# A retention and two expert layers on one core: the slots of the first layer's ranked experts worked out over six steps of the first job, where one step held them all

## The chip, the core and the metric

The kernel runs on one core of a Trainium2 chip. The metric is device time in microseconds (us), the median of several runs. Engines are named as the profile names them: PE is TensorE, DVE is VectorE, ACT is ScalarE, POOL is GpSimd, SP is the engine that issues most transfers. PEld is PE's loading of weights.

## What is computed

A linear attention with decay (2 x 8 heads, 768 positions, 64 wide) gives 1536 tokens of 512 numbers. Two layers of eight experts follow. Each token goes to its two best experts in the first layer, weighted by a softmax of the two logits, and to its best one in the second, up to a capacity:

```python
noisy_logits = x @ w_gate + np.log1p(np.exp(x @ w_noise)) * noise
top2 = np.argpartition(-noisy_logits, 2, axis=1)[:, :2]
...
h = np.maximum(x[mask] @ w1[e], 0.0)
out[mask] += top2_w[mask, k, None] * (h @ w2[e])
```

In the second layer `expert_idx = np.argmax(x @ w_gate, axis=1)`, and the output of the expert is multiplied by the softmax probability.

## The kernel before, in words

The core works through jobs. A job is one expert with a number of its tokens: it gathers their rows by an indirect DMA from POOL, turns them by PE transposes (`tr`, L730), splits them into a high and a low part (L731 on ACT, L732 on DVE), and multiplies by split weights, three matmuls (L740, L741, L742) for each product of two tiles. A job of the first kind has nine steps. In step f PE sums eighth f + 1 of the first product into a PSUM bank `hp` (12 matmuls here), ACT takes its relu (L814), DVE takes the relu's low part (L815, which the change's title calls a relu too), and PE adds eighth f of the second product into `yp` (12 matmuls again). The matmuls L741 of the second product read what L815 wrote. `experts` runs these steps, and behind each step calls `extra1(j, i)` with the job's and the step's number, where other work can be put in.

The first layer's job 0 is expert 0 with up to 288 of the tokens of the first nine tiles, whose choice is known early. Job 1 is expert 0 with up to 128 tokens of the rest. Jobs 2 to 8 are the other seven experts, ranked by the number of their tokens, with 408 to 372 slots each. Which token stands in which of these slots is worked out by `slots`: for 24 groups of 128 choices (12 tiles of tokens, two choices each) DVE finds rank and row of every choice and spreads the values to be placed over the columns that they may go to (`sel`, L433, then one large product, L442). 24 short instructions (L445, called marks below) set a one-hot tile for each group. 24 small matmuls (L447) then add the groups up, beginning with the last group. That is done twice, once for the tokens' numbers (into `tr`, from `more`) and once for their weights (from `oh`, in `rest`). DVE turns the sums into `Rsrc` and `Rdst`, by which POOL gathers and scatters, and `Rwt`.

All of this was in `late()`, called behind step 1 of job 0. Instructions carry priorities, and the engines' orders are set by them when the program is built: on the chip each engine takes its own list strictly in order. `tc.issue_after(tail[...])` ranks what stands in it behind the last instruction of that kind.

Two buffers matter. `flat`, which holds `sel` and the ranks, is the same buffer as `yT`, into which ACT and DVE copy a job's output when it ends (L876, L874, before the matmuls L892). `tr` has two banks, used in turn by transposes, by L892 and by both runs of L447.

Of the kernel before, what the change touches and what calls it, by code (L numbers as in the profile page):

```python
# [14 lines left out]
OP = mybir.AluOpType  # L15
# [22 lines left out]
def kernel(ctx: ExitStack, tc: tile.TileContext, q, k, v, lam, g1, gn, noise,  # L38
# [375 lines left out]
    def slots(nm, rank, row, nh, flat, lows_, first_, last_, choices, tag, past):  # L414
# [5 lines left out]
        for x, w in (("ge", nh + 1), ("up", 1), ("lo", 1), ("hi", nh), ("ro", RANKED), ("sel", C)):  # L420
# [3 lines left out]
        nc.vector.tensor_tensor(ge, rank[:, :, None].to_broadcast([P, K, nh + 1]),  # L424
                                steps_p[:, None, :nh + 1].to_broadcast([P, K, nh + 1]), op=OP.is_ge)
        nc.vector.tensor_reduce(up[:, :, 0], ge, axis=AX.X, op=OP.add)

        nc.vector.scalar_tensor_tensor(lo[:, :, 0], up[:, :, 0], -float(P), rank, op0=OP.mult, op1=OP.add)
        nc.vector.tensor_scalar(lo[:, :, 0], lo[:, :, 0], P + 1.0, None, op0=OP.add)
        nc.vector.tensor_sub(hi, ge[:, :, :nh], ge[:, :, 1:])  # L430
        nc.vector.tensor_tensor(ro, row[:, :, None].to_broadcast([P, K, RANKED]),
                                e_up[:, None, :RANKED].to_broadcast([P, K, RANKED]), op=OP.is_equal)
        nc.vector.tensor_tensor(sel.rearrange("p k (r h) -> p k r h", h=nh),  # L433
                                ro[:, :, :, None].to_broadcast([P, K, RANKED, nh]),
                                hi[:, :, None, :].to_broadcast([P, K, RANKED, nh]), op=OP.mult)
        src, dst, wt = small(nm + "src", [P, C], I32), small(nm + "dst", [P, C], I32), small(nm + "wt", [P, C])

        def columns(values, rhs, make):
            f = values.shape[2]
            rhs = rhs[:, :K * f * C].rearrange("p (k f c) -> p k f c", k=K, f=f)  # L440
            ps = bank(tag, [P, 3, RANKED * 4])[:, :f, :C]
            nc.vector.tensor_tensor(rhs, sel[:, :, None, :].to_broadcast([P, K, f, C]),  # L442
                                    values[:, :, :, None].to_broadcast([P, K, f, C]), op=OP.mult)
            for k in range(K if make else 0):
                nc.vector.tensor_scalar(lows_(k), slot1[:, :P], lo[:, k, :], None, op0=OP.is_equal)  # L445
            for i, k in enumerate([K - 1, *range(K - 1)]):
                nc.tensor.matmul(ps, lows_(k), rhs[:, k], start=(i == 0), stop=(i == K - 1))  # L447
            return ps

        ps = columns(first_[0], first_[1], True)  # L450
        t, ch, d = (small("sl" + x, [P, 2 * NT + 4])[:, :C] for x in "tcd")
        nc.vector.tensor_copy(t, ps[:, 1])
        nc.vector.scalar_tensor_tensor(d, t, 0.0, past, op0=OP.is_equal, op1=OP.max)
        nc.vector.tensor_scalar(d, d, 2.0 * NO_SLOT, None, op0=OP.mult)
        if choices:
            nc.vector.tensor_scalar(ch, t, 16.0, None, op0=OP.is_gt)
            nc.vector.scalar_tensor_tensor(t, ch, -16.0, t, op0=OP.mult, op1=OP.add)
        nc.vector.scalar_tensor_tensor(t, t, float(P), ps[:, 0], op0=OP.mult, op1=OP.add)
        picked = nc.vector.tensor_scalar(src, t, -float(P), 0.0, op0=OP.add, op1=OP.max).ins
        if choices:  # L460
            nc.vector.scalar_tensor_tensor(t, t, 2.0, ch, op0=OP.mult, op1=OP.add)
        nc.vector.scalar_tensor_tensor(dst, t, (-2.0 if choices else -1.0) * P, d, op0=OP.add, op1=OP.add)

        def rest():
            ps = columns(last_[0], last_[1], False)
            nc.vector.tensor_reduce(wt, ps.rearrange("p f c -> p c f"), axis=AX.X, op=OP.add)
# [8 lines left out]
        return of, rest, dst, picked  # L475
# [604 lines left out]
    def late():  # L1080
# [312 lines left out]
```

## Time and profile before

| what | value |
|---|---|
| device time, median of 3 runs | 638.32 us (638.04 to 640.14) |
| the profiled execution, its own time | 643.0 us |
| its span in the trace | 641.2 us |
| mean granted clock of PE over the span | 0.986 |
| PE busy | 603.7 us, 94% of the span |
| DVE busy | 375.1 us, 58% |
| ACT busy | 279.8 us, 44% |
| POOL busy | 175.0 us, 27% |

The profiled execution is one run with the profiler on; the time around its span is 1.8 us. PE's busy time is that of its records. Stretches of the program are named by microseconds from the span's start: the attention fills the time up to about 94 us, job 0 runs from there to 134.8 us, job 1 to about 152 us, the ranked jobs follow, and the second layer begins at about 450 us.

### The profile page before, as it was taken

The numbers are of one execution on the slowest core, as the hardware profiler recorded it, in microseconds if no ns is written. First come the engines' busy times: TensorE is split into PE (matmuls) and PEld (weight loads), VectorE is DVE, ScalarE is ACT, GpSimd is POOL, SyncE is SP. The second block draws the span as 40 slices with busy tenths as digits, with TensorE's granted clock in tenths as the row PEclk, the third lists the DMA queues.
The fourth block names the chain that finished last, engine by engine and source line by source line (L and its number), as shares of the span: only waits on it lengthen the run. The fifth ranks groups of instructions, "written<-read, shape, count | busy, mean of one in ns | idle before, by whom it ended". The sixth has DMA issues, their size and how long they took to land. (4 is left out here: it accounts for less than half of the span.)

```text
span 641.2 us, 11321 instructions
## 1 busy us (share of the span) xinstructions
PE 603.7 (94%) x4173; PEld 562.0 (88%) x4173; DVE 375.1 (58%) x841; ACT 279.8 (44%) x486; POOL 175.0 (27%) x255
## 2 busy tenths in 40 slices
PE   3999989799999999999999999989989999998896
PEld 3898878788999999999999999978669989987795
DVE  3475859736545454464644545447867668557881
ACT  2466531035443353343534434136136357366762
POOL 3844620245004021040310101032255035032101
PEclk9999999799999999999999999999989999999999
DMA  6799522437736447466543421182497977867620
GB/s 151 172 302 270 150 87 86 133 110 253 244 103 211 132 131 231 137 212 183 171 168 98 151 67 51 27 282 84 158 300 244 287 233 227 266 209 239 209 79 33
DMA packets 106048, 110.34 MB, mean 172 GB/s; under 512 B 35855, under 2 KB 81951, under 8 KB 105984
## 3 DMA queue, kind: packets, MB, share of 16 engines
q1 hardware_dynamic: 97920, 83.58, 43.3%
q0 software_dynamic: 8064, 25.95, 12.0%
q8 instruction: 35, 0.57, 0.4%
q14 instruction: 29, 0.24, 0.1%
HBM read 92.48 MB, written 18.79 MB: 174 GB/s over the span
## 5 line engine op out<-in xcount | busy, mean ns | idle before, releaser
L112 DVE TENSOR_TENSOR wl<-wst,wh 128x1024 fp32r<-128x1024 f32 x107 | 135.1, 1270 | 58.1 <-ACT wh L106 56.5
L106 ACT CAST wh<-wst 128x1024 fp32r<-128x1024 f32 x107 | 111.3, 1047 | 32.6 <-PE yp L741 27.1
L740 PE MATMUL hp<-x,wh 128*128 128x372 f32 (+9 forms) x352 | 116.2, 331 | 0.8 <-ACTq L1232 0.4
L741 PE MATMUL hp<-x,wh 128*128 128x372 f32 (+9 forms) x352 | 116.2, 331 | 0.0
L742 PE MATMUL hp<-x,wl 128*128 128x372 f32 (+9 forms) x352 | 115.3, 328 | 0.0
L814 ACT ACTIVATE h<-hp 128x372 fp32r<-128x372 f32 (+9 forms) x88 | 41.2, 469 | 165.6 <-PE hp L742 151.7
L740 PE MATMUL yp<-h,wh 128*128 128x372 f32 (+8 forms) x320 | 106.4, 334 | 1.3 <-ACT h L814 1.3
L742 PE MATMUL yp<-h,wl 128*128 128x372 f32 (+8 forms) x320 | 107.0, 334 | 0.0
L741 PE MATMUL yp<-h,wh 128*128 128x372 f32 (+8 forms) x320 | 106.5, 333 | 0.1
L815 DVE SCALAR_TENSOR_TENSOR h<-hp,h 128x372 fp32r<-128x372 f32 (+9 forms) x88 | 46.5, 528 | 70.3 <-ACT h L814 67.7
L740 PEld LDWEIGHTS hp<-x,wh 128*128 128x128 f32 x352 | 66.2, 188 | 1.9 <-ACTq L1232 0.7
L741 PEld LDWEIGHTS hp<-x,wh 128*128 128x128 f32 x352 | 66.3, 189 | 0.4
L742 PEld LDWEIGHTS hp<-x,wl 128*128 128x128 f32 x352 | 66.2, 188 | 0.1
L490 POOL DMA_INDIRECT xg<-x,Rsrc x25 | 24.3, 971 | 142.0 <-PE tr L730 123.9
L741 PEld LDWEIGHTS yp<-h,wh 128*128 128x128 f32 x320 | 60.8, 190 | 0.7 <-DVE h L815 0.5
L740 PEld LDWEIGHTS yp<-h,wh 128*128 128x128 f32 x320 | 60.0, 188 | 1.5 <-ACT h L814 1.5
L742 PEld LDWEIGHTS yp<-h,wl 128*128 128x128 f32 x320 | 60.7, 190 | 0.3 <-issue 0.2
L732 DVE TENSOR_TENSOR x<-tr,x 128x128 fp32r<-128x128 f32 (+12 forms) x72 | 29.1, 436 | 35.9 <-ACT x L731 35.4
L927 POOL DMA_INDIRECT x<-y,Rdst x25 | 24.9, 998 | 81.7 <-DVE y L901 77.7
L731 ACT CAST x<-tr 128x128 fp32r<-128x128 f32 (+12 forms) x72 | 25.8, 387 | 39.4 <-PE tr L730 38.4
L892 PE MATMUL tr<-iw,yT 128*128 128x136 f32 (+2 forms) x224 | 34.2, 288 | 0.4 <-issue 0.4
L500 POOL TENSOR_TENSOR xg<-xg 128x512 f32<-128x512 f32 (+1 forms) x16 | 22.4, 1403 | 41.0 <-DMA xg<-x,Tsrc 21.6
(370 smaller groups left out, 1036.7 us busy)
## 6 DMA issues: line engine op xcount, KB each, us to landing
wst<-in_moe_w_dram SPq DMA_DIRECT2D x107, 512.0 KB
more<-in_moe_w_dram SPq DMA_DIRECT2D x21, 512.0 KB
ldk<-in_k_dram SPq DMA_DIRECT2D x12, 256.0 KB
ldq<-in_q_dram SPq DMA_DIRECT2D x6, 512.0 KB
ldv<-in_v_dram SPq DMA_DIRECT2D x12, 256.0 KB
x<-xr SPq DMA_DIRECT2D x12, 256.0 KB
out_dram<-zero SPq DMA_DIRECT2D x12, 256.0 KB
dm<-powers SPq DMA_DIRECT2D x1, 512.0 KB
```

The lines of the kernel that those rows point to most:

```text
L106: nc.scalar.copy(hi, st)
L112: nc.vector.tensor_sub(lo, st, hi.bitcast(F32))
L490: i = nc.gpsimd.indirect_dma_start(out=r, out_offset=None, in_=x, in_offset=bass.IndirectOffsetOnAxis(ap=src(s)[:m], axis=0))
L731: a = nc.scalar.copy(hi[:, d, :n], ps[:, :n])
L732: v_ = nc.vector.tensor_sub(lo[:, d, :n], ps[:, :n], hi[:, d, :n].bitcast(F32))
L740: nc.tensor.matmul(ps, a[0], b[0], start=start, stop=False)
L741: nc.tensor.matmul(ps, a[0], b[1], start=False, stop=False)
L742: tail["pe"] = nc.tensor.matmul(ps, a[1], b[0], start=False, stop=stop).ins
L814: tail["act"] = nc.scalar.activation(hh, ps, AF.Relu).ins
L815: tail["dve"] = nc.vector.scalar_tensor_tensor(hl, ps, 0.0, hh.bitcast(F32), op0=OP.max, op1=OP.subtract).ins
L892: nc.tensor.matmul(ps[:m, i, :], self.yT[:, 2 * b + i, s * r:s * r + m], iw[:, 2 * b + i, gates2], start=True, stop=True)
L927: i = nc.gpsimd.indirect_dma_start(out=target, out_offset=bass.IndirectOffsetOnAxis(ap=dst, axis=0), in_=y, in_offset=None, bounds_check=t ...
```

## The change

`slots` no longer runs its parts itself; it returns them as functions: `pick` (ranks, rows and `sel`), `spread` for the first values, `mark` for some of the groups, `head` (the first 24 matmuls and what DVE makes of them), `spread` for the weights, and `rest`. `late(i)` is called behind steps 1 to 7 of job 0 and does one of them at a time; the weights' matmuls come in step 0 of job 1. The second layer calls the same parts one behind the other, in the order that it had.

```diff
-        def columns(values, rhs, make):
+        def spread(values, rhs):
+            f = values.shape[2]
+            return nc.vector.tensor_tensor(view(values, rhs), sel[:, :, None, :].to_broadcast([P, K, f, C]),
+                                           values[:, :, :, None].to_broadcast([P, K, f, C]), op=OP.mult).ins
+
+        def mark(ks):
+            for k in ks:
+                i = nc.vector.tensor_scalar(lows_(k), slot1[:, :P], lo[:, k, :], None, op0=OP.is_equal)
+            return i.ins
+
+        def columns(values, rhs):
             f = values.shape[2]
-            rhs = rhs[:, :K * f * C].rearrange("p (k f c) -> p k f c", k=K, f=f)
             ps = bank(tag, [P, 3, RANKED * 4])[:, :f, :C]
-            nc.vector.tensor_tensor(rhs, sel[:, :, None, :].to_broadcast([P, K, f, C]),
-                                    values[:, :, :, None].to_broadcast([P, K, f, C]), op=OP.mult)
-            for k in range(K if make else 0):
-                nc.vector.tensor_scalar(lows_(k), slot1[:, :P], lo[:, k, :], None, op0=OP.is_equal)
             for i, k in enumerate([K - 1, *range(K - 1)]):
-                nc.tensor.matmul(ps, lows_(k), rhs[:, k], start=(i == 0), stop=(i == K - 1))
+                nc.tensor.matmul(ps, lows_(k), view(values, rhs)[:, k], start=(i == 0), stop=(i == K - 1))
             return ps
...
-        return of, rest, dst, picked
+        return of, dst, pick, lambda: spread(*first_), mark, head, lambda: spread(*last_), rest
...
-        last_rows.append(dst)
-        fetch()
-        fetch()
-        jobs[2].prepare()
-        rest()
-        later1.extend((tot1, rk1))
...
+            fetch()
+            fetch()
+        with tc.issue_after(tail["dve"]), tc.issue_after(tail["pe"]):
+            if i == 2:
+                phases.extend(ranked(later1[1]))
+                phases[2]()
+            if i == 3:
+                phases[3]()
+            if i in (4, 5):
+                phases[4](range(NT) if i == 4 else range(NT, 2 * NT))
+            if i == 6:
+                phases[5]()
+                for r, size in enumerate(FIRST):
+                    jobs.append(Job(("a", r + 1), size, phases[0](r), x1, x2, True, ranked=True))
+                last_rows.append(phases[1])
+                jobs[2].prepare()
+            if i == 7:
+                phases[6]()
...
         if j == 0 and i == 1:
             jobs.append(jobB)
-            late()
+        if j == 0 and 1 <= i <= 7:
+            late(i)
+        if j == 1 and i == 0:
+            with tc.issue_after(tail["pe"]):
+                phases[7]()
```

In the changed kernel the lines have other numbers: L442 is now L446, L445 L451, L447 L458, L740 to L742 are L754 to L756, L815 is L829, L874 L888, L892 L906, L732 L746.

How it moves PE's list, at the place in job 0 where the tokens' matmuls stand. Before, four matmuls of the second product's step 4 (`h_1677`, with `wh12`), then 24 of L447 from `more2` and, right behind, 24 from `oh`:

```order
L740 MATMUL yp0_1323<-h_1677,wh12_82 128x288
L740 MATMUL yp1_1324<-h_1677,wh12_82 128x288
L740 MATMUL yp2_1325<-h_1677,wh12_82 128x288
L740 MATMUL yp3_1326<-h_1677,wh12_82 128x288
L447 LDWEIGHTS more1_1221
L447 MATMUL tr_1487<-more2_1222,more1_1221 128x56
```

Now the rest of that step, the first product's step 6 (`hp_1650`, with `wh03`) and the second product's step 5 (`h_1623`) stand ahead of them, and the first product's step 7 (`hp_1721`) behind; these are the rows around them:

```order
L756 MATMUL hp_1650<-x1_1224,wl03_87 128x288
L754 MATMUL yp0_1323<-h_1623,wh12_82 128x288
L755 MATMUL yp0_1323<-h_1623,wh12_82 128x288
...
L756 MATMUL yp3_1326<-h_1623,wl12_90 128x288
L458 LDWEIGHTS more1_1221
L458 MATMUL tr_1678<-more2_1222,more1_1221 128x56
...
L458 MATMUL tr_1678<-more2_1222,more0_1220 128x56
L754 MATMUL hp_1721<-x1_1224,wh03_79 128x288
```

The 24 matmuls moved back by 32 large ones, of which 8 are the rest of the step that they used to cut in two.

PE's list in job 1, behind the matmuls L906 that finish job 0 (`yT`), where the weights' matmuls now stand (before, only the last L892 and the next matmul stood there):

```order
L906 MATMUL tr_1837<-iw_105,yT_1778 96x136 x2
L756 MATMUL hp_1881<-wh02_78,x0_1223 128x256
L754 MATMUL hp_1881<-wh02_78,x0_1223 128x256
L906 MATMUL tr_1841<-iw_105,yT_1778 96x136 x2
L458 LDWEIGHTS more1_1221
L458 MATMUL tr_1853<-oh_1528,more1_1221 128x84
```

The 24 matmuls from `oh` left job 0 and stand in the middle of job 1's first product.

DVE's list in job 0. Before, all 24 marks and the weights' spread (`oh`) stand ahead of two low parts L815:

```order
L445 TENSOR_SCALAR more1_1221<-slot1_144,yT_1475 128x128
L442 TENSOR_TENSOR oh_1476<-yT_1475,wts_155 128x2016
L452 COPY slt_1537<-tr_1487 128x28
L815 SCALAR_TENSOR_TENSOR h_1677<-hp_1664,h_1677 128x288
L453 SCALAR_TENSOR_TENSOR sld_1539<-slt_1537,past1_161 128x28
L456 TENSOR_SCALAR slc_1538<-slt_1537 128x28
L815 SCALAR_TENSOR_TENSOR h_1705<-hp_1692,h_1705 128x288
```

Now one low part stands ahead of `sel` (L436), one between mark 12 and mark 13, and one behind mark 24; the weights' spread stands behind job 1's splits and ahead of the copies into `yT`:

```order
L829 SCALAR_TENSOR_TENSOR h_1583<-hp_1570,h_1583 128x288
L436 TENSOR_TENSOR yT_1527<-yT_1527 128x672
L451 TENSOR_SCALAR more0_1220<-slot1_144,yT_1527 128x128
L446 TENSOR_TENSOR more2_1222<-yT_1527,who_153 128x1344
...
L829 SCALAR_TENSOR_TENSOR h_1623<-hp_1610,h_1623 128x288
...
L829 SCALAR_TENSOR_TENSOR h_1663<-hp_1650,h_1663 128x288
...
L746 TENSOR_TENSOR x0_1223<-tr_1761,x0_1223 128x128
L446 TENSOR_TENSOR oh_1528<-yT_1527,wts_155 128x2016
L888 COPY yT_1778<-yp1_1324 128x288
```

Three low parts moved ahead of work that they used to stand behind, and the spread of the weights moved behind the last of job 0's low parts.

## Rows read from the trace of the kernel before

**Rows 1.** Windows: span, busy us of each engine (count), granted clock, DMA share, GB/s

```profile
114.76:134.78 20.02, 14.77 (x127) 13.94 (x125) 11.57 (x58) 2.64 (x9) 6.05 (x7) 0.83 0.35 105
134.78:152.00 17.22, 16.96 (x119) 14.79 (x118) 8.27 (x16) 7.81 (x15) 10.47 (x13) 1.00 0.52 169
152.00:450.00 298.00, 295.56 (x1824) 286.33 (x1824) 155.18 (x268) 122.89 (x196) 51.84 (x56) 1.00 0.48 151
```

**Rows 2.** Waits of PE from 80 to 145 us: total, times, longest

```profile
PE tr L447 <- DVE more L445: 3.0, 1, 3.0
PE yp L740 <- ACT h L814: 1.3, 1, 1.3
PE tr L447 <- DVE oh L442: 0.9, 1, 0.9
```

**Rows 3.** Timeline of PE in job 0: start, us, line, tiles, count, idle before

```profile
113.17 0.29 PE L740 MATMUL hp<-x,wh 128*128 128x288 f32 x1
...
114.76 0.69 PE L740 MATMUL yp<-h,wh 128*128 128x288 f32 x4
118.48 1.30 PE L447 MATMUL tr<-more,more 128*128 128x56 bf16 x24 [3.02 <-DVE more L445]
120.64 1.86 PE L447 MATMUL tr<-oh,more 128*128 128x84 bf16 x24 [0.87 <-DVE oh L442]
...
134.78 0.28 PE L740 MATMUL hp<-wh,x 128*128 128x256 f32 x1
...
137.63 1.09 PE L892 MATMUL tr<-iw,yT 128*96 128x136 f32 x8
...
148.17 0.96 PE L730 MATMUL tr<-iw,xg 128*128 128x128 f32 x8
```

**Rows 4.** Windows of 2 us around the wait (columns as in rows 1)

```profile
118.00:120.00 2.00, 1.30 (x24) 1.16 (x24) 2.00 (x4) 0.00 (x0) 0.00 (x0) 0.50 0.00 0
...
124.00:126.00 2.00, 2.00 (x15) 2.00 (x14) 1.09 (x7) 0.00 (x0) 1.39 (x3) 0.83 0.39 94
```

**Rows 5.** Timeline of DVE from 112 to 121 us

```profile
112.20 0.24 DVE L445 TENSOR_SCALAR more<-slot,yT 128x128 bf16<-128x128 f16 x1
112.36 0.85 DVE L433 TENSOR_TENSOR yT<-yT 128x672 f32<-128x672 f32 x1
...
113.29 1.54 DVE L442 TENSOR_TENSOR more<-yT,who 128x1344 bf16<-128x1344 f32 x1
114.76 3.66 DVE L445 TENSOR_SCALAR more<-slot,yT 128x128 bf16<-128x128 f16 x22
118.34 2.25 DVE L442 TENSOR_TENSOR oh<-yT,wts 128x2016 bf16<-128x2016 f32 x1
...
120.60 0.44 DVE L815 SCALAR_TENSOR_TENSOR h<-hp,h 128x288 fp32r<-128x288 f32 x1
```

**Rows 6.** Timeline of ACT: two of job 0's relus and the copies into yT

```profile
111.84 0.41 ACT L814 ACTIVATE h<-hp 128x288 fp32r<-128x288 f32 x1 [5.67 <-PE hp L742]
...
132.04 0.41 ACT L814 ACTIVATE h<-hp 128x288 fp32r<-128x288 f32 x1 [5.33 <-PE tr L730]
...
134.58 0.40 ACT L876 COPY yT<-yp 128x288 f32<-128x288 f32 x1
```

**Rows 7.** Timeline of POOL: the last of job 2's four gathers

```profile
127.19 0.91 POOL L490 DMA_INDIRECT xg<-x,Rsrc  x1 [0.30 <-issue]
```

**Rows 8.** Timeline of DVE at the end of job 0

```profile
134.45 0.48 DVE L732 TENSOR_TENSOR x<-tr,x 128x128 fp32r<-128x128 f32 x2
```

**Rows 9.** Timeline of PE in the second layer: the same small matmuls there

```profile
461.34 0.47 PE L447 MATMUL yp<-yT,more 128*128 128x42 bf16 x12 [1.57 <-DVE more L445]
...
469.94 0.56 PE L447 MATMUL yp<-yT,more 128*128 128x63 bf16 x12
```

**Rows 10.** Windows in the second layer (columns as in rows 1)

```profile
462.60:464.00 1.40, 1.40 (x5) 0.78 (x3) 1.40 (x11) 0.28 (x1) 0.88 (x1) 0.50 1.02 383
...
466.00:469.40 3.40, 3.40 (x22) 2.38 (x20) 1.17 (x2) 0.00 (x0) 0.57 (x1) 0.50 1.09 378
```

More of the change, by code (lines that the diff above doesn't have):

```diff
@@ L430, in slots @@
[L430 to L435, printed above, removed]
@@ L448, in columns @@
             return ps
[L450 to L462, printed above, removed]
+        def head():
+            ps = columns(*first_)
+            t, ch, d = (small("sl" + x, [P, 2 * NT + 4])[:, :C] for x in "tcd")
+            nc.vector.tensor_copy(t, ps[:, 1])
+            nc.vector.scalar_tensor_tensor(d, t, 0.0, past, op0=OP.is_equal, op1=OP.max)
+            nc.vector.tensor_scalar(d, d, 2.0 * NO_SLOT, None, op0=OP.mult)
+            if choices:
+                nc.vector.tensor_scalar(ch, t, 16.0, None, op0=OP.is_gt)
+                nc.vector.scalar_tensor_tensor(t, ch, -16.0, t, op0=OP.mult, op1=OP.add)
+            nc.vector.scalar_tensor_tensor(t, t, float(P), ps[:, 0], op0=OP.mult, op1=OP.add)
+            picked = nc.vector.tensor_scalar(src, t, -float(P), 0.0, op0=OP.add, op1=OP.max).ins
+            if choices:
+                nc.vector.scalar_tensor_tensor(t, t, 2.0, ch, op0=OP.mult, op1=OP.add)
+            nc.vector.scalar_tensor_tensor(dst, t, (-2.0 if choices else -1.0) * P, d, op0=OP.add, op1=OP.add)
+            return picked
@@ L464, in rest @@
         def rest():
-            ps = columns(last_[0], last_[1], False)
+            ps = columns(*last_)
             nc.vector.tensor_reduce(wt, ps.rearrange("p f c -> p c f"), axis=AX.X, op=OP.add)
@@ L1078, with late @@
     later1, last_rows = [], []
[L1080 to L1099 removed]
+    def late(i):
+        if i == 1:
+            with tc.issue_after(tail["pe"]):
+                tot1 = route1("tr")
+                nc.vector.tensor_scalar(rB, r1, doneA, None, op0=OP.subtract)
+                id1, rk1 = by_size("a", tot1, 0)
+                jobB.prepare()
+                selA[3]("tr")
+            later1.extend((tot1, rk1))
+            for r, size in enumerate(FIRST):
+                e = reg(id1, r, E - 1)
+                want(("a", r + 1), w1[ds(e, 1)].rearrange("o d f -> (o d) f"),
+                     w2[ds(e, 1)].rearrange("o f d -> (o f) d"), "aabbaabb" if r == 0 else "abababab")
+            fetch()
[10 more added lines that the diff above has]
+                phases[5]()
+                for r, size in enumerate(FIRST):
+                    jobs.append(Job(("a", r + 1), size, phases[0](r), x1, x2, True, ranked=True))
[3 more added lines that the diff above has]
+                phases[6]()
+    phases = []
     def rows_to_zero():
@@ L1116, in extra1 @@
             jobs.append(jobB)
-            late()
+        if j == 0 and 1 <= i <= 7:
+            late(i)
+        if j == 1 and i == 0:
+            with tc.issue_after(tail["pe"]):
+                phases[7]()
         if j in (4, 5) and 1 <= i <= NT // 2:
@@ L1326, in extra2 @@
                 later.append(rk2)
-                of, rest, _, picked = later[1]
+                of, _, pick, spread1, mark, head = later[1][:6]
+                pick()
+                spread1()
+                mark(range(NT))
+                later.append(head())
                 for k, r in enumerate(TURNS):
@@ L1335, in extra2 @@
         if j == 0 and i == 5:
-            with tc.issue_after(later[1][3]):
+            with tc.issue_after(later[3]):
                 gates()
@@ L1340, in extra2 @@
                 jobT.rest()
-                later[1][1]()
+                later[1][6]()
+                later[1][7]()
             places.append(more[2])
@@ L1350, in settle @@
                 nc.gpsimd.drain()
-    total, body = later[3]
+    total, body = later[4]
     jobs[BEFORE + 3].prepare()
```

32 lines of the change are left out of this document (15 added, 17 removed).

## The prediction

> **What bounds the kernel now.** I read the windows first. In the ranked jobs PE is busy for 295.56 of 298 us, and in job 1 for 16.96 of 17.22, both at a granted clock of 1.00 [rows 1]. So PE's list is the program's length there: what PE gains in job 0 should arrive at the end. In job 0's second half the picture is another one: 14.77 of 20.02 us, at 0.83. PE's waits say why: 3.0 us for the marks of L445, 0.9 for the weights' spread, 1.3 for a relu [rows 2]. The timeline puts the first two where the small matmuls L447 stand: PE has four matmuls behind 114.76 and then stands still until 118.48 [rows 3]. In the windows that follow the granted clock is 0.50, half of its level before, and it is back inside the window 124 to 126 [rows 4]. DVE is busy throughout: from 112.20 on it works through `sel`, the tokens' spread, 22 marks in a row and the weights' spread, and only then, at 120.60, comes the low part of a relu that ACT had started at 111.84 [rows 5, 6]. So PE's list had to cross a block of DVE's work that it could not yet use.
>
> **What is removed, added and moved.** The kind of work and its amount stay the same; the places change.
>
> *PE in job 0, before.* The stretch from 114.76 to 134.78, the first matmul of job 1, is 20.02 us [rows 1, 3]. It holds 72 large matmuls (three steps of the first or second product pair, 24 each), four transposes, and 48 small matmuls. Twelve large ones at full clock take 114.76 - 113.17 = 1.59 us [rows 3], so the 72 take 6 x 1.59 = 9.54. A transpose takes 0.96 / 8 = 0.12 [rows 3], four 0.48. The rest, 20.02 - 9.54 - 0.48 = 10.0 us, is small matmuls (1.30 and 1.86, both at half clock), three waits (3.02, 0.87, 1.3), and 1.65 of slow clock on large matmuls and of restarts.
>
> *PE in job 0, after.* The list from 114.76 on is now 36 large matmuls, 24 small ones, 36 large ones with the transposes among them. The question is whether DVE keeps ahead. The relu at 111.84 ends 0.41 later [rows 6], so the first low part starts on DVE at about 112.3. Behind it stand `sel` 0.85, one mark 0.16, the spread 1.54, and eleven marks; a mark in a row costs 3.66 / 22 = 0.166, so 1.83 [rows 5]. Then the second low part, 0.44, twelve marks, 2.0: 112.3 + 0.44 + 0.85 + 0.16 + 1.54 + 1.83 + 0.44 + 2.0 = 119.55. PE reaches the small matmuls at 114.76 + 3 x 1.59 = 119.53. They meet almost to the tenth; the first small matmul needs the last mark, so I allow 0.1 of a wait. The low parts come in time: the first is done at 112.8 and used from 114.9 on, the second is done at 117.6 and used from about 118.0 on, the third follows the last mark at about 120.0 and is used from 122 on.
>
> *The tokens' small matmuls at full clock* do not stand in this trace with 56 columns. From below: twelve of 42 columns take 0.47, so 24 no less than 0.94, less one pipeline end; I take 0.75 as the lowest, since each record's end is drawn out. From above: the 1.30 of half clock [rows 9, 3]. I take 0.9, nearer to the row at full clock.
>
> So the stretch becomes 9.54 + 0.48 + 0.9 + 0.1 = 11.0 instead of 20.0: a gain of 9.0. PE would begin job 1 at about 125.8.
>
> *Added to job 1.* The weights' 24 matmuls: from below 2 x 0.56 = 1.12 by twelve of 63 columns at full clock, from above the 1.86 of half clock [rows 9, 3]; with 84 columns I take 1.2. They wait for the spread, which is long done by then.
>
> *The spread of the weights and the copies into `yT`.* The spread reads `sel` out of the buffer that the copies write, so ACT's and DVE's copies now stand behind it. Before, the last of job 1's splits started at about 134.65, just ahead of job 1's first matmul at 134.78, and the copies were over by about 135.3 [rows 8, 6], 2.3 ahead of their first use at 137.63 [rows 3]. After, the spread starts some 0.1 behind job 1's first matmul, takes 2.25 [rows 5], and a pair of copies 0.4 to 0.7: 2.8 to 3.1 us behind job 1's start, where L892 stands 137.63 - 134.78 = 2.85 behind it. So the cover is used up and PE waits 0 to 0.3, I take 0.2. From below it is nothing; from above, if the splits come later, the whole spread, 2.25.
>
> *Costed at nothing.* `Rsrc` comes at about 121.8 instead of 122.96, and POOL's four gathers for job 2 ended at 128.1 [rows 7], while its transposes come at 148.17 before [rows 3] and about 140.4 after: 12 us of cover, and without it a lateness would show one for one. The weights' reduction now holds a `tr` bank until DVE has done two splits of job 2's weights; the next matmul that needs this bank stands 0.7 us later by the same sums, and if that is gone PE waits by what is missing, at most the 0.25 of the reduction and a split. The order of SP and POOL does not change, and so no transfer is issued in another turn; each starts earlier with PE.
>
> *The sum.* -9.0 + 1.2 + 0.2 = -7.6 us, against the profiled execution's own 643.0: 635.4. The median of the runs is 638.32, 4.7 below the profiled one, and I cannot see where those 4.7 lie. One candidate stands in the stretch: the relu wait of 1.3. The relu started at 132.04, and the trace names transposes as its releaser [rows 6], which stand a whole step behind the sum that it reads; that is found once in the trace. If runs without the profiler lack this wait, the gain is 6.3. So the median comes to 638.3 - 7.6 = 630.7 or 638.3 - 6.3 = 632.0; I take 631.3. With all bounds at their worst (1.30, 1.86, 2.25 and no relu wait) the gain is 9.0 - 0.4 - 1.3 - 1.86 - 2.25 = 3.2: 635.1; at their best (0.75, 1.12, nothing) 9.2 - 1.1 = 8.1: 630.2.
>
> **The rivals.** A change within 0.3% (1.9 us) is one that this measurement cannot tell from none.
>
> *The wait moves instead of going.* PE and DVE meet within 0.1 us, so any slower DVE shows. A single mark lasts 0.24, not 0.166 [rows 5]; 24 of them at 0.24 end 1.8 us later. If PE waits 1.8 there and the clock falls again, for a stretch as long as the one now, about 118 to 124.5 [rows 4], some 3 us of large matmuls are lost to it: -7.6 + 1.8 + 3 = -2.8, 635.5. Against it: 22 marks do run at 0.166, and a low part between them reads nothing of theirs. The Trainium skill, VectorE: DVE Perf Modes, section The DRAIN you can't avoid, says that the next instruction does not start until the pipe of the one before has emptied, and that one which is not held starts earlier; by the first half of that rule the marks would come at their full length, and the time at this rival's. The trace disagrees for the marks of before, at 0.166 from start to start.
>
> *Another fall of the clock comes or goes.* In the second layer the granted clock is 0.50 from 462.6 to 469.4, behind a wait of only 1.57 us [rows 9, 10]. That costs about half of the 6 us that PE is busy in it, 3 us. Everything there now comes 7 us earlier; if the fall stays away the time is 628.3, if one more comes elsewhere 634.3. The Trainium skill, TensorE: Matmul & The Clock Gate, section What's actually happening, says that the monitor's windows run free and do not begin with the kernel; by that rule the same waits may meet a fall in one run and not in another. No row here can show it, as there is one execution.
>
> *The gain is given back later.* If job 2 had to wait for weights or rows, the earlier start would be a wait there: 638. Against it: PE idles 2.4 of 298 us in all that follows job 1 in the first layer [rows 1], and the splits that free the staging buffers follow PE's own steps.
>
> *Slower.* The relu wait happened while POOL issued its gathers. After the change the gathers run from about 122 to 129, over the end of job 0 and the change of jobs, where PE, ACT and DVE hand over about ten times. If such a hand-over stalls each time by the 5.33 that ACT stood idle [rows 6], two of them eat more than the gain: -7 + 10.7 = 642. Two is the point from which it decides. Against it: one in the whole trace, and more gathers and scatters ran after 134 us without it.
>
> **How the numbers follow.** The forecast has 0.69; the wait that moves 0.09; the clock elsewhere 0.10 (half either way); given back 0.06; slower 0.06. The range must leave out no more than 0.2: from 628.3, where the second fall stays away, to 635.5, the moved wait. Faster by over 0.3% (below 636.4) are the forecast, the clock cases and the moved wait, the last only just: 0.86. Same: 0.08. Slower: 0.06.
>
> **What would show it.** Right: no wait at the first small matmuls, granted clock 1.00 from 114 to 126, job 1's first matmul at 125 to 126.5, a run of 24 matmuls from `oh` some 4 us behind it that takes 1.1 to 1.4, and the time from there to the end unchanged but for that. Wrong: a wait for marks above 1 us with a clock of 0.50 behind it (the marks), a wait of L906 for `yT` above 0.5 (the spread), or a gap at job 2's start.

## The result, and the profile after

The changed kernel took 632.02 us (median of 5 runs, 631.28 to 634.14) where the kernel before took 638.32 beside it: a ratio of 0.9901, 95% interval 0.9883 to 0.9919. The forecast was 631.3. That is the answer of one chip. On two others, met in the experiments, the same two programs stand the other way round, at 1.0022 (1.0008 to 1.0036) and 1.0021 (1.0001 to 1.0040). Both answers are traced below; why the chips differ stays open.

First the profile of the run that was forecast. Windows of the changed kernel, cut at the fifth product of job 0, at job 1 and at job 2 (span, then busy us of PE, PEld, DVE, ACT, POOL, then the granted clock), answering to [rows 1]:

```profile
115.39:126.18 10.79, 10.79 (x103) 10.58 (x101) 9.18 (x57) 2.18 (x7) 2.74 (x3) 1.00 0.28 89
126.18:140.62 14.44, 14.18 (x119) 12.50 (x118) 8.93 (x14) 6.18 (x11) 11.53 (x13) 1.00 0.68 197
140.62:630.80 490.18, 471.88 (x3030) 446.53 (x3028) 284.36 (x522) 223.18 (x379) 114.36 (x107) 1.00 0.54 176
```

PE's timeline at the places of [rows 3]:

```profile
120.14 0.79 PE L458 MATMUL tr<-more,more 128*128 128x56 bf16 x24
120.77 0.38 PE L754 MATMUL hp<-x,wh 128*128 128x288 f32 x1
...
126.18 0.28 PE L754 MATMUL hp<-wh,x 128*128 128x256 f32 x1
...
129.02 1.09 PE L906 MATMUL tr<-iw,yT 128*96 128x136 f32 x8
...
132.79 1.08 PE L458 MATMUL tr<-oh,more 128*128 128x84 bf16 x24
133.70 0.36 PE L755 MATMUL hp<-wl,x 128*128 128x256 f32 x1
...
140.62 0.96 PE L744 MATMUL tr<-iw,xg 128*128 128x128 f32 x8
```

No row has an idle time before it: the small matmuls found their marks ready, and the clock is 1.00 in the stretch where [rows 4] showed 0.50. DVE's timeline, answering to [rows 5]:

```profile
115.69 1.87 DVE L451 TENSOR_SCALAR more<-slot,yT 128x128 bf16<-128x128 f16 x11
117.47 0.45 DVE L829 SCALAR_TENSOR_TENSOR h<-hp,h 128x288 fp32r<-128x288 f32 x1
117.84 2.03 DVE L451 TENSOR_SCALAR more<-slot,yT 128x128 bf16<-128x128 f16 x12
119.79 0.45 DVE L829 SCALAR_TENSOR_TENSOR h<-hp,h 128x288 fp32r<-128x288 f32 x1
...
126.09 2.25 DVE L446 TENSOR_TENSOR oh<-yT,wts 128x2016 bf16<-128x2016 f32 x1
```

The low part behind the last mark starts at 119.79, and PE arrives at 120.14: a slack of 0.35 us (0.27 from the end of the last mark's record, 117.84 + 2.03). ACT and POOL at the change of jobs:

```profile
128.37 0.70 ACT L890 COPY yT<-yp 128x288 f32<-128x288 f32 x2 [2.52 <-DVE oh L446]
```

```profile
125.33 0.95 POOL L504 DMA_INDIRECT xg<-x,Rsrc  x1 [0.30 <-PE tr L744]
126.59 2.54 POOL L504 DMA_INDIRECT xg<-x,Rsrc  x1 [0.30 <-issue]
```

ACT's copies waited 2.52 us for the weights' spread, as foreseen, and PE still had no wait at L906, which reads them from 129.02 on.

### The profile page after: what moved, and what is told of

It is laid out like the page before. It is cut to its first block, busy times and chain, and to the rows that moved or that the text cites. A ratio compares the mean times of both kernels' runs of the same rounds, so it can differ in the third digit from the quotient of the medians.

```text
span 630.8 us, 11323 instructions
## 1 busy us (share of the span) xinstructions
PE 598.5 (95%) x4173; PEld 558.7 (89%) x4173; DVE 373.1 (59%) x841; ACT 279.8 (44%) x486; POOL 180.1 (29%) x255
## 5 line engine op out<-in xcount | busy, mean ns | idle before, releaser
L754 PE MATMUL hp<-x,wh 128*128 128x372 f32 (+9 forms) x352 | 116.1, 330 | 0.8 <-ACTq L1264 0.4
L756 PE MATMUL hp<-x,wl 128*128 128x372 f32 (+9 forms) x352 | 115.3, 328 | 0.0
L754 PE MATMUL yp<-h,wh 128*128 128x372 f32 (+8 forms) x320 | 106.9, 334 | 0.0
L756 PE MATMUL yp<-h,wl 128*128 128x372 f32 (+8 forms) x320 | 106.3, 332 | 0.0
L829 DVE SCALAR_TENSOR_TENSOR h<-hp,h 128x372 fp32r<-128x372 f32 (+9 forms) x88 | 46.4, 527 | 62.9 <-ACT h L828 62.6
L754 PEld LDWEIGHTS hp<-x,wh 128*128 128x128 f32 x352 | 66.1, 188 | 1.9 <-ACTq L1264 0.7
L756 PEld LDWEIGHTS hp<-x,wl 128*128 128x128 f32 x352 | 66.1, 188 | 0.1
L504 POOL DMA_INDIRECT xg<-x,Rsrc x25 | 26.4, 1057 | 136.0 <-PE tr L744 118.8
L756 PEld LDWEIGHTS yp<-h,wl 128*128 128x128 f32 x320 | 60.2, 188 | 0.2 <-issue 0.2
L754 PEld LDWEIGHTS yp<-h,wh 128*128 128x128 f32 x320 | 60.2, 188 | 0.0
L746 DVE TENSOR_TENSOR x<-tr,x 128x128 fp32r<-128x128 f32 (+12 forms) x72 | 29.2, 436 | 38.0 <-ACT x L745 37.5
L514 POOL TENSOR_TENSOR xg<-xg 128x512 f32<-128x512 f32 (+1 forms) x16 | 24.7, 1546 | 39.3 <-DMA xg<-x,Tsrc 24.4
L906 PE MATMUL tr<-iw,yT 128*128 128x136 f32 (+2 forms) x224 | 34.2, 287 | 0.0
```

What stands on the lines that cost most here:

```text
L504: i = nc.gpsimd.indirect_dma_start(out=r, out_offset=None, in_=x, in_offset=bass.IndirectOffsetOnAxis(ap=src(s)[:m], axis=0))
L746: v_ = nc.vector.tensor_sub(lo[:, d, :n], ps[:, :n], hi[:, d, :n].bitcast(F32))
L754: nc.tensor.matmul(ps, a[0], b[0], start=start, stop=False)
L756: tail["pe"] = nc.tensor.matmul(ps, a[1], b[0], start=False, stop=stop).ins
L829: tail["dve"] = nc.vector.scalar_tensor_tensor(hl, ps, 0.0, hh.bitcast(F32), op0=OP.max, op1=OP.subtract).ins
L906: nc.tensor.matmul(ps[:m, i, :], self.yT[:, 2 * b + i, s * r:s * r + m], iw[:, 2 * b + i, gates2], start=True, stop=True)
```

## The experiments

They ran in three sets of four, each set on another chip, and within a set beside the kernel before. They are read by the same three stretches as above. The first ends at job 1, the second at job 2's transposes, the third at the end.

### First set: the halves of the change, and the clock alone

**The kernel before, once more.** No edit.

> The kernel before, once more, with the granted clock of every run. If the profile of before was an ordinary execution, PE waits 3.0 us for the marks in job 0 again, the clock of 0.50 follows it again, and the time is 638.3. The second fall, at 462.6 to 469.4 us in the one profile of before and absent in the one of after, is the open point: if it belongs to the kernel before, the profile shows it again; if it comes and goes with the execution, it is missing in some, and the run without it is about 3 us shorter. The wait of 1.3 us for a relu late in job 0, seen once: if it is an accident of one execution it is gone.

**The weights alone moved.** All that belongs to the tokens stays in one step.

```diff
+                phases.extend(ranked(rk1))
+                phases[2]()
+                phases[3]()
+                phases[4](range(2 * NT))
+                phases[5]()
...
+        if i == 7:
+            with tc.issue_after(tail["dve"]), tc.issue_after(tail["pe"]):
+                phases[6]()
```

> The kernel before with only the second half of the change: the weights' spread and their 24 matmuls leave job 0, as in the changed kernel, and everything for the tokens stays in the one step behind step 1. Theory (the gain is the distance between marks and matmuls, the weights' part is small change): PE still waits 3.0 us for the marks and the clock still falls; what goes is the wait for the spread, 0.87, and 1.86 of slow small matmuls, and 0.9 comes back in job 1. That is -1.8 us: 636.5, and 636 to 637 with what the low parts gain. Rival (the long weights' spread was what held DVE's low parts up, so that most of the gain is in taking it out of job 0): -4 or more, 634 or below. Rival (weights do not matter): 638.3.

**The weights put back into job 0.** The tokens alone in steps.

```diff
                 jobs[2].prepare()
-            if i == 7:
                 phases[6]()
+                phases[7]()
...
-        if j == 1 and i == 0:
-            with tc.issue_after(tail["pe"]):
-                phases[7]()
```

> The changed kernel with the weights' spread put right behind the tokens' sums in job 0, and their 24 matmuls ahead of the last matmul of step 7's first product: the tokens' part alone in steps. Theory: the marks' end at 119.8 and a low part of 0.45 are followed by the spread of 2.25, which ends at 122.5; PE comes to its matmuls at about 122.2, waits 0.3, and spends the same 0.9 there that it spends in job 1 now: 632.3, no difference that can be told from the changed kernel, and ACT's copies into yT no longer wait for the spread. Rival (moving the weights to job 1 is a good part of the gain): a wait of 1 us or more and a fall of the clock behind it, 634 to 636.

**The kernel before with its waits filled.** The added matmuls write the bank that the real ones overwrite.

```diff
+            for k in (range(2, K - 2) if make else [0] * 8) if choices else []:
+                with tc.issue_after(tail["sum"] if not make else tail["pe"]): fill(all_, lows_(k))
```

> The kernel before with matmuls of no use in PE's waits: 20 of 384 columns, each for one of the marks, ahead of the tokens' small matmuls, and 8 ahead of the weights'. Nothing is taken from DVE, so PE gets to the end of the weights' spread at 120.6 as before. It parts the 9 us that the stretch lost into waiting and slow clock. Theory (the clock falls because PE stands still for 3 us): the granted clock stays at 1.00 from 114 to 126; the weights' matmuls take 0.9 in place of 1.86 and the large ones behind them no longer cost 1.6 more: -2.5 us, 635.8, with a first matmul of job 1 at about 132. Rival (the clock falls because of the small matmuls, or at that time whatever PE does): 0.50 is still there, and the time is 638.3. The other 4 us of the gain would be the wait itself, which this kernel keeps.

Measured: before once more 638.93 (ratio 1.0018, 1.0001 to 1.0035), weights moved 636.82 (0.9978, 0.9959 to 0.9997), weights back 632.64 (0.9916, 0.9894 to 0.9938), waits filled 636.78 (0.9977, 0.9961 to 0.9993). The windows of these four, one kernel to a fence:

```profile
116.83:135.33 18.50, 14.61 (x127) 14.09 (x125) 11.67 (x58) 2.78 (x9) 6.05 (x7) 0.82 0.38 115
135.33:148.73 13.40, 13.13 (x95) 11.53 (x94) 6.40 (x12) 5.69 (x10) 8.45 (x10) 1.00 0.47 140
148.73:638.50 489.77, 471.73 (x3030) 446.46 (x3028) 283.18 (x522) 223.30 (x379) 110.61 (x106) 1.00 0.54 175
```

```profile
115.12:130.58 15.46, 12.44 (x102) 12.06 (x101) 8.88 (x56) 2.17 (x7) 6.00 (x7) 0.89 0.43 133
130.58:145.02 14.44, 14.17 (x118) 12.52 (x117) 8.94 (x15) 6.18 (x11) 10.33 (x11) 1.00 0.51 163
```

```profile
114.28:126.11 11.83, 11.82 (x127) 11.53 (x126) 11.42 (x58) 2.51 (x8) 2.59 (x3) 1.00 0.25 81
126.11:139.50 13.39, 13.12 (x94) 11.52 (x93) 6.59 (x13) 5.78 (x11) 10.47 (x13) 1.00 0.71 200
```

```profile
115.49:131.91 16.42, 16.42 (x155) 14.21 (x153) 11.68 (x58) 2.78 (x9) 6.04 (x7) 1.00 0.42 120
131.91:145.32 13.41, 13.14 (x94) 11.52 (x93) 6.40 (x12) 5.68 (x10) 8.47 (x10) 1.00 0.50 150
```

Four things follow. First, the relu wait of 1.3 us [rows 2] is gone from the second profile of before, whose first stretch is 18.50 and not 20.02; the wait of 3.02 is the same to the hundredth:

```profile
120.55 1.30 PE L447 MATMUL tr<-more,more 128*128 128x56 bf16 x24 [3.02 <-DVE more L445]
```

So against this profile the change gains 18.50 - 10.79 = 7.71 in job 0, gives 14.44 - 13.40 = 1.04 back in job 1 and 490.18 - 489.77 = 0.41 in the rest: 6.3, which is what the medians say. (The spans of the two profiles lie 7.7 apart. The other 1.44 us stand ahead of the stretch, where this profile of before has a clock of 0.50 from 94 to 98 us and the changed kernel has 1.00.)

Second, the weights' matmuls cost the same in job 0 and in job 1 once the tokens' part is in steps (11.83 - 10.79 = 1.04 us in job 0, 14.44 - 13.39 = 1.05 in job 1): moving them then gains nothing. With the tokens' part in one step it gains 18.50 - 15.46 - 1.04 = 2.0, as the wait for the spread goes and half of the slow clock; the wait of 3.02 stays. The 636.5 that was expected came as 636.82. Third, with the waits filled PE is never idle in the stretch, the clock stays at 1.00, and 18.50 becomes 16.42: 2.1 us of the loss were slow clock, brought on by the waiting. I had expected 2.5. Fourth, what is left between 16.42 and the changed kernel's 10.79 + 1.04 is 4.6 us, the waits themselves (more than 3.02 and 0.87, because at full clock PE reaches the second wait earlier). The distance between marks and matmuls is the gain, about 7 parts in 10 as waiting and 3 as clock.

### Second set: the price of lateness, and another chip

**The changed kernel again.** No edit.

> The changed kernel once more, with the granted clock of every run. In the first profile the clock stayed at 1.00 from 19.65 us to the end. If the change took away a cause of falls in job 0 and only there, PE waits for no mark again, the stretch from the fifth product's start to job 1 is 10.8 us again, and the time is 632.0, while falls elsewhere (at 93 us, in the second layer) come in one run and not in another and spread the runs by 1 to 3 us. If the first profile was lucky, this one shows a fall in job 0 or a wait, and the median lies nearer to 634.

**The second twelve marks written twice, and three times.** The first product of step 7 is held behind the tokens' matmuls. The diff is that of twice; the other has 3 for the 2.

```diff
-                phases[4](range(NT) if i == 4 else range(NT, 2 * NT))
+                for _ in range(1 if i == 4 else 2):
+                    phases[4](range(NT) if i == 4 else range(NT, 2 * NT))
             if i == 6:
                 phases[5]()
+                pinned.append(tail["sum"])
...
+            if pinned:
+                with tc.issue_after(pinned.pop()):
+                    product()
```

> The changed kernel with the second twelve marks written twice over (the same tiles, the same numbers), and the first product of step 7 held behind the tokens' 24 matmuls, so that the list of PE does not give way. DVE is later by 12 x 0.166 = 2.0 us. PE has four large matmuls more ahead of the small ones, 0.53, and there was a slack of 0.35, so it waits about 1.1 us. Theory (lateness is paid one to one, and a wait of this size costs no clock): 632.0 + 1.1 = 633.1. Rival (any wait here is followed by a fall of the clock, which the kernel with filled waits prices at 1.7): 634.8. Second rival (DVE's time in this block is hidden anyhow): 632.0.

> The same with the twelve marks written three times: DVE later by 4.0 us, PE waits about 3.1 us, as long as in the kernel before (3.02), but with the other parts of the change in place. Theory that the wait and its clock are the gain: 632.0 + 3.1 + 1.7 = 636.8, with a clock of 0.50 behind the wait as in the kernel before. Rival (a wait alone, the clock having fallen in the kernel before for another reason): 635.1 at a clock of 1.00. Rival (hidden): 632.0.

**The second layer's gates later.**

```diff
-        if j == 0 and i == 5:
-            with tc.issue_after(later[3]):
+        if j == 0 and i == 8:
+            with tc.issue_after(tail["dve"]):
                 gates()
```

> The changed kernel with the same thought applied to the second layer: its gates (L1300 to L313), and the small matmuls for the weights there, now come behind the splits of that layer's job 1 and not ahead of them; the output is scaled from the same numbers. In the changed kernel's profile PE waits 1.23 us for aux and 0.40 for job 1's first rows there, and DVE is busy without a break from 446 to 457.6 us. Theory (PE's list there is bound by DVE work that it does not need yet): these waits go, the small matmuls of some 2.9 us only change places, so -1.2 to -1.6: 630.6. Rival (the wait of 1.60 for the marks and the low parts behind it hold the stage, and the waits come back at the matmuls that need aux): 632.0. Rival on the other side (the scaled output or the gathers come too late for the job behind): 633 or more.

Measured: the changed kernel 643.92 (1.0022, 1.0008 to 1.0036, to a kernel before that took 642.41 here), marks twice 645.69 (1.0060, 1.0041 to 1.0079), marks three times 646.22, gates later 642.03 (0.9999, 0.9978 to 1.0019). The executions with the marks three times fall into two groups, four at 637.8 to 640.8 and eight at 645.6 to 650.1, so that no ratio is read from its median. The profiled one, 637.8, is of the lower group.

The price of lateness is read from the first stretch, which is 10.79 again for the changed kernel here. Windows of the kernels with the marks twice and three times, each with the row of its wait, and of the second the clock around it:

```profile
115.41:127.42 12.01, 10.94 (x102) 10.57 (x101) 10.85 (x69) 2.18 (x7) 2.49 (x3) 1.00 0.24 80
```

```profile
121.92 0.79 PE L458 MATMUL tr<-more,more 128*128 128x56 bf16 x24 [1.07 <-DVE more L451]
```

```profile
115.35:130.84 15.49, 12.48 (x102) 12.11 (x101) 12.77 (x81) 2.17 (x7) 3.74 (x4) 0.89 0.24 68
...
122.00:124.00 2.00, 0.21 (x8) 0.21 (x9) 2.00 (x12) 0.00 (x0) 0.00 (x0) 1.00 0.00 0
124.00:126.00 2.00, 2.00 (x32) 2.00 (x29) 2.00 (x19) 0.00 (x0) 0.00 (x0) 0.77 0.00 0
126.00:128.00 2.00, 2.00 (x10) 2.00 (x10) 1.04 (x9) 0.41 (x1) 1.50 (x2) 0.50 0.12 18
```

```profile
123.79 0.79 PE L458 MATMUL tr<-more,more 128*128 128x56 bf16 x24 [3.01 <-DVE more L451]
```

PE waited 1.07 us in the first of these, at a clock of 1.00 throughout, and the stretch grew by 1.22: lateness is paid about one to one. In the second it waited 3.01, the clock fell behind the wait, and the stretch grew by 4.70: 3.0 of wait and 1.7 of clock. Both theories were right, each at its size of wait; the times expected with them do not apply here, since the medians of this set hold something else as well.

By its median the kernel with the gates later is 1.9 us faster than the changed kernel beside it, though the intervals of their two ratios overlap. PE's wait for `aux` in the second layer is 0.3 there, and 1.2 in the first profile of the changed kernel, as expected:

```profile
PE tr L377 <- DVE aux L313: 0.3, 1, 0.3
```

```profile
PE tr L377 <- DVE aux L313: 1.2, 1, 1.2
```

Of the 12 us that the changed kernel lost against its first run, 10 are in the second stretch and 2.3 in the third:

```profile
125.62:150.11 24.49, 16.89 (x119) 14.42 (x118) 8.98 (x14) 6.18 (x11) 14.66 (x16) 0.79 0.54 166
150.11:642.60 492.49, 473.33 (x3030) 447.80 (x3028) 284.18 (x522) 223.15 (x379) 110.67 (x103) 0.99 0.54 172
```

Job 1 takes 24.49 us in place of 14.44, by the same program. PE's rows there, then ACT's and DVE's that depend on them:

```profile
132.24 1.08 PE L458 MATMUL tr<-oh,more 128*128 128x84 bf16 x24
...
138.42 0.43 PE L756 MATMUL hp<-wh,x 128*128 128x256 f32 x1
...
145.54 0.69 PE L850 MATMUL tr<-iw,hr 128*128 128x128 f32 x2 [5.85 <-ACT hr L843]
```

```profile
144.90 0.60 ACT L843 ACTIVATE hr<-hp 128x512 f32<-128x512 f32 x1 [10.82 <-remote]
```

```profile
140.51 0.25 DVE L480 TENSOR_REDUCE Rwt<-tr 128x28 f32<-128x84 f32 x1 [4.26 <-PE tr L850]
```

ACT's relu reads what PE is recorded to have finished at 138.85, and starts at 144.90; DVE's reduction reads what the 24 matmuls finished at 133.32, and starts at 140.51 after an idle time of 4.26. In the first profile of the changed kernel the same relu started 0.04 behind its matmul (136.31 and 136.35):

```profile
136.35 0.60 ACT L843 ACTIVATE hr<-hp 128x512 f32<-128x512 f32 x1 [1.72 <-PE hp L756]
```

So the others go on some 6 us behind PE's recorded end, and PE then waits for them.

The traces also hold the updates of the semaphores, the counters by which one engine tells another that it is done, and these say whose delay it was. (The word `remote` in ACT's row means that no recorded instruction ended closely before such an update.) PE's semaphore was counted up at 133.15, next at 140.49, next at 144.87; DVE and ACT started 0.02 and 0.03 us behind the last two. Neither was slow to start: PE's signal came late, or its matmul ended later than recorded, which the trace cannot part. In the first profile of the changed kernel and in the four of the first set each of the 1819 to 1842 updates of PE, DVE and ACT stands within 0.03 us of the recorded end of its instruction. In each profile of the other two chips 64 to 91 of them stand over 0.4 us behind it or are missing, and every one of these belongs to an instruction that ends within 1.5 us of an indirect transfer's issue on POOL. Of all the updates, late or not, only four in ten do. The first profile of before has 74 of them.

POOL had issued its eight gathers by 133.52. It went on with seven scatters, and ACT's start at 144.90 came 1.4 us behind the end of the last:

```profile
142.52 0.98 POOL L1134 DMA_INDIRECT x<-y,Rdst  x1 [0.30 <-issue]
```

In the three other profiles with the weights' matmuls and a late relu in job 1 the same distance is 1.4 us (1.37 to 1.45), and in the two with the weights back 1.9 and 2.0. Yet DVE's start at 140.51 came in the middle of such a row. What the late signals have in common is thus POOL's indirect transfers, scatters as well as gathers; how these hold them up is not shown.

Ahead of that wait PE's own product already has gaps of 0.2 to 0.5 us, 1.65 in sum from 134 to 138, that the profile puts down to nothing but issue, and the clock is at half from 138 on, so here it falls behind these gaps and not behind the long wait:

```profile
138.00:140.00 2.00, 1.60 (x8) 1.09 (x6) 0.00 (x0) 0.00 (x0) 1.39 (x3) 0.54 0.89 252
140.00:142.00 2.00, 0.00 (x0) 0.00 (x0) 0.25 (x1) 0.00 (x0) 1.70 (x2) 0.50 1.00 396
...
146.00:148.00 2.00, 2.00 (x8) 1.71 (x7) 1.32 (x2) 0.58 (x1) 0.00 (x0) 0.50 0.00 0
```

By the windows of the stretch PE is idle for 24.49 - 16.89 = 7.6 us, where it was idle for 14.44 - 14.18 = 0.3, and busy for 16.89 - 14.18 = 2.7 more: of the 10 us, 7.3 are waits and gaps and 2.7 slow clock. The late relu of before [rows 6], at 132.04 and 2.6 us behind its matmul, is of this kind. It came 1.4 us behind the end of a row of six gathers:

```profile
129.66 0.95 POOL L490 DMA_INDIRECT xg<-x,Rsrc  x1 [0.30 <-issue]
```

The chip alone does not decide what this costs. The profile with the marks three times, on this same chip, has 81 late or missing signals, but no long late start in job 1, which took 15.41 us at a clock of 1.00:

```profile
130.84:146.25 15.41, 14.71 (x119) 12.63 (x118) 8.98 (x14) 6.18 (x11) 12.49 (x13) 1.00 0.66 209
```

That execution, which lost 4.7 us more in job 0, was faster than all twelve of the changed kernel beside it. So, as far as this one profile shows, the cost hangs on whether something waits for a late signal. No execution of its upper group was profiled.

### Third set: what the late starts hang on

**The changed kernel a third time**, and **the weights back** once more (their edits as above).

> The changed kernel a third time, because its two profiles disagree: in the first it took 632.0 us, in the second, on another chip, 643.9 with the same program. In the second, ACT's relu hr in job 1 starts 6.05 us behind the recorded end of the matmul that it waits for, and the clock then falls for 10.2 us; the profile of before, too, has such a late start (2.6 us, at 132.04), and five other profiles have none at all. Theory (some chips do this to every program here while POOL issues gathers, and others never): the time is either 632 with no late start in the profile and -1.0% to the kernel before on the same chip, or about 644 with one and slower than the kernel before. Rival (chance of a single set of executions): something between, and both kinds of execution in one set.

> The changed kernel with the weights' part back in job 0, once more, beside the changed kernel on the same chip. Where no late start happens: within 0.3% of the changed kernel, 632.6. Where they happen: the late start in job 1 came at the 24 matmuls from oh, in the middle of job 1's first product, so if that place is what makes it cost 6 us, this kernel loses less, some 636 to 638; if the gathers alone set it, it loses the same and takes 644.

**Plain loads in place of eight gathers.** Jobs 2 and 3 work on other rows, the second layer's routing becomes another, and only the time up to job 2 is to be read.

```diff
+            if plain:
+                i = nc.sync.dma_start(r, x[s * P:s * P + m, :])
+            else:
+                i = nc.gpsimd.indirect_dma_start(out=r, out_offset=None, in_=x,
...
+                self.g = gather(self.src, self.n, self.rows, self.source, self.key in (("a", 1), ("a", 2)))
```

> The changed kernel with the eight gathers of rows for jobs 2 and 3 replaced by plain loads of as many rows that SP issues; these two jobs then work on other rows than the choices name. POOL issues no indirect transfer between 112 and 133 us. Where late starts happen, theory (POOL's issuing holds up PE's completions): none at all in job 0 and the first two thirds of job 1, and 632. Rival (the traffic or the chip alone): the late start and the 644 stay. Where none happen: 632, as the rows come early in both.

**Weights back and gates later together.**

> Both variants in one: the weights' part back in job 0 and the second layer's gates behind its job 1's splits, which took 1.9 us less than the changed kernel on the same chip (642.03 against 643.92) and whose profile there has a wait of 0.3 for aux where the changed kernel had 1.2. Theory: 1.4 to 1.9 below the kernel with the weights back alone, 631 where no late start happens. Rival (the gates' gain was a matter of the late starts): the same time as with the weights back alone.

Measured: the changed kernel 644.44 (1.0021, 1.0001 to 1.0040, to 642.33 before), weights back 640.47 (0.9973, 0.9954 to 0.9993), both variants 637.90 (0.9938, 0.9915 to 0.9961). The plain loads make 762.36 of the whole, with which nothing is compared. Job 1 in these four, in the order of the expectations:

```profile
125.90:150.83 24.93, 16.40 (x119) 14.26 (x117) 8.99 (x15) 6.18 (x11) 14.70 (x16) 0.86 0.52 163
```

```profile
126.77:145.50 18.73, 13.78 (x94) 11.72 (x93) 6.85 (x14) 6.22 (x12) 12.24 (x14) 1.00 0.55 164
```

```profile
125.70:141.59 15.89, 14.35 (x118) 12.51 (x117) 8.94 (x14) 6.29 (x11) 8.30 (x10) 1.00 0.55 169
```

```profile
128.78:147.56 18.78, 15.24 (x94) 13.20 (x93) 6.75 (x13) 6.05 (x11) 12.20 (x14) 0.91 0.54 155
```

The changed kernel repeats its loss, 24.93, of it 8.5 idle; the clock of this one falls only inside the long wait (1.00 up to 142, 0.50 at 144). Without the eight gathers job 1 takes 15.89, 1.45 more than where no late start happens, and ACT's relu starts 1.17 behind its matmul (it ends at 135.84), while POOL is issuing scatters:

```profile
137.01 0.60 ACT L847 ACTIVATE hr<-hp 128x512 f32<-128x512 f32 x1 [2.86 <-PE tr L854]
```

```profile
130.76 0.97 POOL L945 DMA_INDIRECT x<-y,Adst  x1 [20.02 <-DVE y L919]
...
136.87 0.99 POOL L1138 DMA_INDIRECT x<-y,Rdst  x1 [0.30 <-issue]
```

So the long late start goes when POOL's fifteen indirect transfers in a row become seven; the theory's "none at all" was too much. That it takes gathers is not shown, since the relu's delay of 6.05 ran while POOL issued scatters. Whether it is POOL's issuing or the transfers that it starts, this run does not part. The weights back took 640.47, between the 636 to 638 of one expectation and the 644 of the other: job 1 loses 18.73 - 13.39 = 5.3 and not 10: there are late starts, but no 24 matmuls whose sum DVE must fetch in the middle of the product, and the clock does not fall. (In the fourth, with the gates later too, it falls for a short while, 0.91, and the stretch is as long.) Both variants together are 4.4 us faster than the kernel before and 6.5 faster than the changed one on this chip. The gates later are worth 640.47 - 637.90 = 2.6 there, above the 1.4 to 1.9 of the theory, and the executions of the two kernels overlap. On a chip without late starts the two variants together were not run.

## Why the prediction held, and where it did not

**The stretch in job 0** was put at 11.0 us and is 10.79 or 10.78 on each of the three chips. The meeting of DVE and PE within a tenth came out as a slack of 0.35, and the marks keep their 0.17 from start to start in rows of eleven and twelve. By the Trainium skill (VectorE: DVE Perf Modes, section The DRAIN you can't avoid), taken at its first half, they would have come at 0.24 each; the trace disagrees again (1.87 for eleven, where 0.24 each would be 2.64).

**What it was 20.02 in place of.** The 9.0 us held the relu wait of one profile. I had said that without it the gain is 6.3 and the median 632.0, and that is what came. The 4.7 us that I could not place have a place now: the profile of before has a late start, and its own time of 643.0 lies among the 639.9 to 645.5 of the kernel before on the second and third chips, and outside its 636.5 to 641.9 on the first. Its 74 late or missing signals, where the profiles of the first set have none, say the same: it came from a chip of the other kind than the runs, or from one that then behaved like it. Its chip was not noted.

**The weights' matmuls and the copies** in job 1 were put at 1.2 and 0.2, 1.4 together. The matmuls take 0.91 (132.79 to 133.70), and job 1 grew by 1.04 in all (14.44 in place of 13.40). L906 stands 2.84 behind job 1's start, where it stood 2.85: PE did not wait. The run of 24 stands 6.6 us behind job 1's start, not "some 4".

**Costed at nothing: the gathers.** This step failed outside of the forecast's chip. Their cover of 12 us against coming late did hold (11.5: the fourth was issued by 129.13, and the transposes came at 140.62). What I gave no price was what they do to others while they run, because the cover hid only their own time. The rival *slower* had the mechanism, a hand-over that stalls while POOL issues, but its size of 5.33 was luck: that was ACT's idle time, and the relu came 2.6 behind its matmul, where 6.05 was measured in the changed kernel. Its "one in the whole trace" counted one wait; the same trace has 74 late or missing signals, which from 152 us on cost PE nothing that shows (489.20 - 471.13 = 18.1 us idle, and 489.77 - 471.73 = 18.0 in the second profile of before, which has none). And it needed two stalls to decide. One such stall of the job's products was enough, since gaps and the slow clock come with it: 10 us in job 1. In the profile of before the gathers fell beside job 0's products, and the one late relu cost PE 1.3 us [rows 2]; POOL's indirect transfers there pause twice, from 130.61 to 134.42 and from 136.59 to 139.85. In the changed kernel they run without such a pause from 122.27 to 143.51, over the change of jobs and one more sum for DVE to fetch. A chance of 0.06 for it fitted the chip of the result and was wrong as a statement on the kernel; that the result came from such a chip was luck.

**The wait that moves** did not come. Its price was half right: a wait of 1.07 costs itself and no clock, one of 3.01 costs 1.7 of clock more, where I had taken 3 behind 1.8.

**A fall elsewhere.** The second layer's wait for its marks is 1.5 to 1.6 us in the three profiles that I read for it; before has 0.50 behind it [rows 9, 10], the second profile of before and the changed kernel have 1.00:

```profile
450.00:475.00 25.00, 21.42 (x172) 17.51 (x171) 20.01 (x96) 5.55 (x12) 8.64 (x8) 1.00 0.73 240
```

```profile
441.00:466.00 25.00, 21.36 (x166) 17.26 (x167) 19.99 (x100) 4.53 (x12) 6.81 (x7) 1.00 0.70 230
```

The same wait meets a fall in one execution and not in another, as the Trainium skill has it (TensorE: Matmul & The Clock Gate, section What's actually happening: the monitor's windows run free). It is a likely part of why the runs of the changed kernel spread by 3 us, but no run here parts it from the rest.

**Given back later** did not happen, but for 0.4: 490.18 from job 2 to the end, 489.77 before.

## What to carry to other kernels

Work that DVE prepares for PE belongs several products ahead of the matmuls that read it, in pieces between the pieces that PE needs at once; measure the distance against PE's list, since a long wait is paid a second time in clock (here those of 3 us were, one of 1.6 in one profile of three, and one of 1.07 not). Where a profile's own time lies outside its runs' range, find out what that execution had and they had not before a gain is summed against it. And before hand-overs between engines are moved under indirect transfers, try both orders on more than one chip: the order that is best without late starts lost 1.5 to 2 us with them.

## What the runs showed of the hardware

On two of the chips, ACT started up to 6.05 and 6.75 us behind the recorded end of the matmul that it waited for, while POOL issued indirect transfers one behind the other, and PE's semaphore was counted up only then; 64 to 91 signals a profile came over 0.4 us late or are missing there. In the changed kernel's first profile and in the four of the first set all came within 0.03 us. Why chips differ in this is open, and it was not tried on a smaller program. One gather took 2.54 us in place of 0.95 beside DVE's spread of 2.25, hidden here. And PE kept its clock through a wait of 1.07 us, and lost half of it behind those of 3.01 and 3.02.
